# Threshold attention and a SoLU feed-forward on one Trainium2 core: the weights' blocks moved slot by slot instead of unit by unit

## The chip, the core and the metric

The kernel runs on one NeuronCore of one Trainium2 chip. Times are device microseconds of one execution. The engines are named as the profile names them: PE (TensorE matmuls, with PEld for its weight loads), DVE (VectorE), ACT (ScalarE), POOL (GpSimd), and SP (SyncE), which here does nothing but issue DMAs. Each engine works through its own queue of instructions in order; where one needs something of another engine or of a DMA, it waits on a semaphore, and all that stands behind it on that queue waits with it.

## The reference: what is computed

There are 8 batches with 8 heads of 576 positions and 64 columns. All is float32, except that `w_in` and `w_out` reach the kernel as 64-bit floats and are rebuilt by it as float32.

```
scores = q @ k^T / 8                               # per head, 576 x 576
scores = where(scores >= max(scores) - tau, scores, -1e9)
attn   = exp(scores - max) / (sum + 1e-9)
x      = (attn @ v), heads side by side            # 4608 tokens x 512
h      = x @ w_in                                  # 4608 x 1024
solu   = h * softmax(h)
ln     = (solu - mean) / sqrt(var + 1e-6) * g_ln
out    = ln @ w_out                                # 4608 x 512
```

## The kernel before

**Slots, units and rounds.** A *slot* is one step of attention on 128 rows of scores for each of two heads. A batch has 18 slots: for each of `kind` 0 and 1 and each pair of heads `hp` 0 to 3 two slots, `r` = 0 and 1, and at the end of the batch two slots of `kind` 2 with the 64 left-over rows of all heads. There are 144 slots. Two slots that share (batch, kind, hp) make a *unit*; a unit's weights are multiplied with `v` together. The program is one long list written out by the loop that starts in line 914, the scheduler of the toolkit being told to keep that order (line 846). Each turn of the loop is a *round*; round s computes the scores of slot s. Below, unit n is the one with slots 2n and 2n+1, so units 0 to 8 are batch 0, and 9 to 17 are batch 1.

**What a round issues, in order.** First the scores on PE (`scores`, line 437, 16 matmuls), the row maxima on DVE (`maxes`, line 458), thresholding and exponential on ACT (lines 473 and 482). Then `normalise` of the slot of the round before on POOL (lines 489 to 492), and jobs that have become due, among them `ff_norm2` (line 713) and `ff_swap` (line 724): a token tile of the feed-forward, normalised by ACT into `V` and by DVE into `u`, has two quarters exchanged by four SP transfers `V<-u`. Next comes the large PE step of the round. It is a quarter of the feed-forward, in a cycle of four rounds: `h` first half, `h` second half (line 642, 32 matmuls each), `o` first half, `o` second half (line 747, 64 each). Rounds with an `h` step can also take the weights-times-`v` step of one unit (`attend_steps`, line 558, 72 matmuls, written `pv`); rounds with an `o` step take none. After this, `blocks` of the slot of the round before: DVE turns the weights in 32x32 blocks (line 517) and SP moves them. Last in a round come the late jobs, among them `ff_turn` (line 734), in which DVE turns `V` into `uT`: in the steady cycle `ff_swap` stands in the first `h` round, `ff_turn` in the second, and the `o` step of the round after that reads `uT` as its stationary operand. Then come the flips and loads of later `q` and `k` (lines 186 to 189 and 168) and loads of `v` (line 151), all on SP.

**Which rounds multiply a unit.** `pv` of unit n is due in round 2n+4, in a few places one later (line 788), but it is taken in the next `h` round. In batches 2 to 7 the four-round cycle fits the units: of two units, one is taken 3 and one 4 rounds after its second slot. In batch 1 the cycle is not yet in step, and four units, 9, 11, 14 and 16, are taken 5 rounds after their second slot (rounds 24, 28, 34 and 38), just before, in program order, the blocks of the second slot of the unit two further on.

**The tiles T and wT.** `T` holds the turned weights, `wT` the same after the transfers that gather from each quarter of the partitions the halves that `pv` needs. `T` has two buffers of 9216 bytes per partition, `wT` two of the same size, so the transfers of unit n+2 write the buffer that `pv` of unit n reads, and must wait for it. There are two forms:

- batch 0, kinds 0 and 1 (`by_slot`): each slot's half of `T` is moved at once, by one transfer of 288 KB (line 512) and two of 144 KB (line 514), in packets of 2304 bytes. The `wT` buffer is taken at the first slot.
- everything else: DVE fills T with both slots, and only after the second are both moved together, by one transfer of 576 KB and two of 288 KB (lines 526 and 528), or, for kind 2, four of 288 KB (line 533), in packets of 4608 bytes. The `wT` buffer is taken at the second slot.

The functions that the diff touches and what calls them:

Of the kernel before, what the change touches and what calls it, by code (L numbers as in the profile page):

```python
# [8 lines left out]
F32 = mybir.dt.float32  # L9
# [7 lines left out]
P = 128  # L17
# [3 lines left out]
def kernel(  # L21
# [27 lines left out]
    nc = tc.nc  # L49
# [7 lines left out]
    NB = S // 32  # L57
    SCALE = -0.125
    BIG = 3.0e38
    ROWS = (slice(0, 64), slice(64, P))  # L60
# [4 lines left out]
    work = ctx.enter_context(tc.tile_pool(name="work", bufs=2))  # L65
# [24 lines left out]
    NK = S // 64  # L90
# [6 lines left out]
    units = {}  # L97
# [6 lines left out]
    def take(name):  # L104
        tag = pairs_free.pop(0)
        return tag, ps_mm.tile([P, 1024], F32, tag=tag, name=name)
# [76 lines left out]
    def turn_natural(i, nm, a):  # L183
# [3 lines left out]
        for j in range(2):  # L187
            nc.sync.dma_start(
                out=pair(i + j)[nm + "T"][:, 32 * NK * a : 32 * NK * (a + 1)],
                in_=flip[ROWS[j]].rearrange("p g t x -> p g (t x)"),  # L190
            )

    def constants(spread):
        ones = work.tile([P, P], F32, tag="T", name="ones")
        nc.gpsimd.memset(ones[0:1], 1.0)
        nc.gpsimd.memset(lims[0], 0.0)
        nc.scalar.activation(out=ntau, in_=lims[0], func=AF.Exp)
        make_identity(nc, ident)
        nc.gpsimd.memset(mhalf, -0.5)
        nc.gpsimd.memset(mone, -1.0)  # L200
        nc.gpsimd.memset(zero, 0.0)
        for l, e in zip(lims, (916, 896)):
            nc.gpsimd.memset(l, -e * 8388608.0)

        nc.tensor.matmul(out=spread, lhsT=ones[0:1], rhs=tau_row, start=True, stop=True)
        nc.vector.tensor_scalar(
            out=scl, in0=spread, scalar1=0.0, scalar2=SCALE, op0=ALU.is_ge, op1=ALU.mult
        )  # L210
        nc.vector.tensor_scalar(
            out=tau_t, in0=spread, scalar1=0.0, scalar2=104.0, op0=ALU.max, op1=ALU.min
        )
        nc.vector.tensor_scalar(out=ntau, in0=tau_t, scalar1=-1.0, scalar2=None, op0=ALU.mult)
# [141 lines left out]
    def source(i):  # L356
        b, hp = divmod(i, NP)
        return halves[b, hp // 2], 2 * (hp % 2)

    def pair(i):  # L360
        if i not in pairs:
            qT = heads.tile([P, S], F32, tag="qT", bufs=6, name="qT")
            pairs[i] = dict(
                qT=qT,
                kT=heads.tile([P, S], F32, tag="kT", name="kT"),
                qe=heads.tile([P, ST], F32, tag="qe", name="qe"),
            )
        return pairs[i]
# [18 lines left out]
    def keep(room, i, nm, ms, by_act):  # L387
        of = room[:, 0 : 64 * len(ms)].rearrange("p (m x a) -> p m a x", a=2, x=32)
        to = pair(i)[nm + "T"].rearrange("p (a m x) -> p m a x", a=2, m=NK)[:, ms[0] : ms[-1] + 1]
        if nm == "k":  # L390
# [21 lines left out]
    live = {}  # L412
# [83 lines left out]
    def blocks(s):  # L496
        b, kind, hp, r = slots[s]
        key = (b, kind, hp)
        if r == 0:
            by_slot = b == 0 and kind < 2  # L500
            dims = [P, 2, NB, 2, 32] if by_slot else [P, NB, 2, 2, 32]
            units[key] = dict(T=work.tile(dims, F32, tag="T", name="T"), by_slot=by_slot)
        u = units[key]
        T = u["T"]
        if u["by_slot"]:
            for h, w in enumerate(live.pop(s)["w"]):
                nc.vector.transpose(out=T[:, r, :, h], in_=w)  # L507
            if r == 0:
                u["wT"] = work.tile([P, 2, 2, NK, 2, 32], F32, tag="wT", bufs=2, name="wT")
            of = T[:, r].rearrange("p (c m) h x -> p c (m h x)", c=2)  # L510
            to = u["wT"][:, r].rearrange("p g m h x -> p g (m h x)")
            nc.sync.dma_start(out=to[:, 1], in_=of[32:96])
            for half in range(2):
                nc.sync.dma_start(out=to[ROWS[half], 0], in_=of[96 * half : 96 * half + 32])
            return
        for h, w in enumerate(live.pop(s)["w"]):
            nc.vector.transpose(out=T[:, :, r, h, :], in_=w)  # L517
        if r == 0:
            return


        T = T.rearrange("p (c m) r h x -> p c (m r h x)", c=2)
        u["wT"] = wT = work.tile([P, 2, NK, 2, 2, 32], F32, tag="wT", bufs=2, name="wT")
        to = wT.rearrange("p g m r h x -> p g (m r h x)")
        if kind < 2:
            nc.sync.dma_start(out=to[:, 1], in_=T[32:96])
            for half in range(2):
                nc.sync.dma_start(out=to[ROWS[half], 0], in_=T[96 * half : 96 * half + 32])
            return
        for g in range(2):  # L530
            for half in range(2):
                of = 64 * half + 32 * g
                nc.sync.dma_start(out=to[ROWS[half], g], in_=T[of : of + 32])

    def attend_steps(key):
        b, kind, hp = key
        unit = units[key]
        wT = unit["wT"].rearrange("p r g m h x -> p g m r h x") if unit["by_slot"] else unit["wT"]  # L540
        unit["y"] = take("pv")
        _, y = unit["y"]
        y = y.rearrange("p (u n) -> p u n", u=2)

        for e in range(2) if kind == 2 else [None]:
            for m in range(NK):
                for u in range(2):
                    d, h0 = source(b * NP + (hp if e is None else e + 2 * u))
                    for h in range(2):
                        if e is None:  # L550
                            to = y[ROWS[h], u, 0:P].rearrange("p (g r x) -> p g r x", r=2, g=2)
                            rhs = wT[ROWS[u], :, m, :, h]
                        else:
                            to = y[ROWS[h], u, 64 * e : 64 * e + 64].rearrange(
                                "p (g x) -> p g x", g=2
                            )
                            rhs = wT[ROWS[u], :, m, e, h]
                        nc.tensor.matmul(  # L558
                            out=to,
                            lhsT=d["v"][  # L560
                                ROWS[u], (h0 + h - u) % 4, m,
                            ],
                            rhs=rhs,
                            start=m == 0, stop=m == NK - 1,
                        )
                        yield
# [248 lines left out]
    for i in range(2 * NP, NPAIR, 2):  # L815
        b, hf = divmod(i // 2, 2)
# [3 lines left out]
        for nm, pieces_at in zip("qk", ats):  # L820
            for a, at in enumerate(pieces_at):
                at += PER * b
                if b == 2:
                    of = at - 3 - (at in (PER + 7, PER + 9))
                else:
                    of = (at - 3) // 4 * 4
# [19 lines left out]
    with tc.manual_schedule():  # L846
# [16 lines left out]
        weight_load(5, nc.sync)  # L863
        tags, tiles = zip(take("tp"), take("tp"))
        constants(tiles[1][:, 1022:1023])
        turn(tiles[0], 0, "k", range(NK))
        turn(tiles[1], 0, "q", range(4))
# [46 lines left out]
        while True:  # L914
# [92 lines left out]
            if attending is not None and attending[1] == 2 and step is not None:  # L1007
                beside = attend_steps(attending)
# [23 lines left out]
            if attending is not None:  # L1032
                for _ in beside or attend_steps(attending):
                    pass
                attended(attending)
                b, kind, hp = attending
                if kind == 2 and b % 2:
                    ready.append((rnd + 1, [(b // 2,)]))
                elif kind < 2 and hp == NP - 1:
                    ready.append((rnd + 1, [(b, kind, 0), (b, kind, 1)]))  # L1040
            if rnd - 1 in live:
                blocks(rnd - 1)
# [10 lines left out]
            if rnd in pieces:  # L1053
                x = pieces[rnd]
# [52 lines left out]
```

## Time and profile before

| | |
|---|---|
| time, median of 3 runs | 855.23 us (852.27 to 858.17) |
| the profiled execution | 853.01 us, of which the span of the profile is 851.2 us |
| PE busy | 818.8 us (96%) |
| DVE / ACT / POOL busy | 675.2 / 568.7 / 496.3 us |
| DMA, queue of SP | 77298 packets, 165.82 MB, 76.9% of 16 engines' span |
| mean granted TensorE clock | 0.987 |

A busy share is a union of an engine's instructions; DMA shares are the mean of the 16 DMA engines. The rows of groups give line, engine, operation, out<-in and count, then busy time, the mean of one in ns, and the idle time before it with what ended it. A timeline row gives start and duration in us; neighbouring instructions of one kind are merged and counted. Rows with SPq are DMA issues on SP's queue: their duration is the time that SP spent on issuing, and the transfer itself lands later.

### The profile page before, as it was taken

What the parts mean: (1) busy time and instruction counts of PE and PEld (TensorE: products, weight loads), DVE (VectorE), ACT (ScalarE), POOL (GpSimd) and SP (SyncE); (2) the same over time, 40 slices, a digit from 0 to 9 for tenths busy, and PEclk for the clock granted to TensorE, in tenths of its full rate; (3) what the DMA queues carried; (4) which work ended last, traced back from release to release, by engine and by line L of the source; (5) the groups of instructions that cost most, each with busy time, mean ns of one, the idle gap of its engine ahead of it and who ended that gap; (6) DMA issues with size and microseconds to landing.
All of it is one profiled execution on the core that took longest, in us unless ns stands there. A gap on an engine that the chain in (4) does not pass through costs nothing.

```text
span 851.2 us, 36155 instructions
## 1 busy us (share of the span) xinstructions
PE 818.8 (96%) x15363; PEld 625.6 (73%) x15363; DVE 675.2 (79%) x1229; ACT 568.7 (67%) x1123; POOL 496.3 (58%) x945
## 2 busy tenths in 40 slices
PE   6779999999999999999999999999999999999997
PEld 5456678678688777777677777777788888887655
DVE  5999887888788888888688888888888888776461
ACT  6878776867566667666677766666666667775221
POOL 4887646666556556565566666565666655555120
PEclk8899999999999999999999999999999999999999
DMA  9998797888888788887878878987888787655312
GB/s 337 265 260 236 198 223 210 222 220 210 220 225 204 192 208 205 226 214 182 204 184 227 219 176 199 234 210 194 213 202 233 200 187 176 165 135 136 68 39 63
DMA packets 77746, 168.54 MB, mean 198 GB/s; under 512 B 11530, under 2 KB 33042, under 8 KB 77586
## 3 DMA queue, kind: packets, MB, share of 16 engines
q1 hardware_dynamic: 77298, 165.82, 76.9%
q8 instruction: 120, 1.97, 1.0%
q10 hardware_dynamic: 288, 0.43, 0.2%
q14 instruction: 40, 0.33, 0.1%
HBM read 46.14 MB, written 9.44 MB: 65 GB/s over the span
## 4 chain that ended last, share of the span: by engine, by line
PE 84%; DVE 4%; DMA 4%; ACT 2%; issue 2%; POOL 1%; SPq 1%; DVEq 0%; ACTq 0%
PE o_ps L747 28%; PE h_ps L642 22%; PE s_ps L437 15%; PE pv L558 14%; PE h_ps L632 3%; DMA wT<-T 2%; DMA raw<-in_moe_w_out_dram 1%; DVE w L458 1%; PE tp L374 1%; ACT w L473 1%; DVE T L507 1%; SPq L724 1%; ACT w L482 1%; DVE bs L687 1%; DMA k<-in_k_dram 0%
## 5 line engine op out<-in xcount | busy, mean ns | idle before, releaser
L747 PE MATMUL o_ps<-w,uT 64*64 64x256 f32 x4608 | 272.1, 378 | 3.2 <-issue 2.6
L473 ACT ACTIVATE w<-s_ps,nth 128x576 f32<-128x576 f32 x280 | 196.9, 738 | 110.8 <-DVE nth L458 93.9
L747 PEld LDWEIGHTS o_ps<-w,uT 64*64 64x64 f32 x4608 | 226.8, 134 | 54.2 <-ACT xh L588 12.1
L458 DVE CUSTOM_DVE_ANT_0 w<-s_ps,tau_t 128x576 f32<-128x576 f32 x280 | 200.0, 751 | 80.6 <-PE s_ps L437 50.9
L492 POOL TENSOR_SCALAR w<-w,sm 128x576 f32<-128x576 f32 x288 | 220.7, 778 | 14.3
L482 ACT ACTIVATE w<-w,ntau 128x576 f32<-128x576 f32 x288 | 219.5, 766 | 0.0
L642 PE MATMUL h_ps<-w,xh 64*64 64x512 f32 x1728 | 205.7, 589 | 0.0
L517 DVE STREAM_TRANSPOSE T<-w 128x576 f32<-128x576 f32 x256 | 184.3, 754 | 20.3 <-POOL w L492 18.3
L558 PEld LDWEIGHTS pv<-wT,v 64*64 64x64 f32 x5760 | 172.0, 134 | 33.4 <-issue 16.4
L437 PE MATMUL s_ps<-kT,qT 64*64 64x64 f32 (+1 forms) x2048 | 175.6, 416 | 14.9 <-ACT w L473 12.6
L558 PE MATMUL pv<-wT,v 64*64 64x128 f32 (+1 forms) x5760 | 172.1, 261 | 3.9 <-DMA wT<-T 2.3
L642 PEld LDWEIGHTS h_ps<-w,xh 64*64 64x64 f32 x1728 | 112.4, 133 | 70.2 <-issue 36.3
L489 POOL TENSOR_SCALAR sm<-sm 128x2 f32<-128x2 f32 x144 | 33.8, 235 | 187.2 <-ACT w L482 183.5
L490 POOL TENSOR_TENSOR sm<-sm,mone 128x2 f32<-128x2 f32 x144 | 107.7, 748 | 12.0
L437 PEld LDWEIGHTS s_ps<-kT,qT 64*64 64x64 f32 x2048 | 72.7, 136 | 23.3 <-ACT w L473 18.5
L588 ACT COPY xh<-pv 128x256 f32<-128x256 f32 x64 | 25.4, 398 | 75.2 <-PE pv L558 75.2
L708 ACT ACTIVATE V<-u,nb,rs 128x1024 f32<-128x1024 f32 x36 | 44.7, 1241 | 40.5 <-POOL nb L698 33.5
L734 DVE STREAM_TRANSPOSE uT<-V 128x1024 f32<-128x1024 f32 x36 | 44.3, 1230 | 17.5 <-DMA V<-u 16.9
L482 ACT ACTIVATION_READ_ACCUMULATOR w<-w,ntau 128x1 f32 x288 | 55.3, 192 | 0.0
L672 DVE TENSOR_TENSOR u<-h_ps,u 128x1024 f32<-128x1024 f32 x36 | 42.8, 1189 | 8.4 <-ACT u L666 8.4
L713 DVE TENSOR_SCALAR u<-u,rs,nb 128x1024 f32<-128x1024 f32 x36 | 34.5, 958 | 17.6 <-ACT V L708 17.6
L687 DVE BATCH_NORM_STATS2 bs<-u 128x6 f32<-128x512 f32 x72 | 46.1, 683 | 0.1
(81 smaller groups left out, 593.1 us busy)
## 6 DMA issues: line engine op xcount, KB each, us to landing
wT<-T SPq DMA_DIRECT2D x160, 288.0 KB, 6.6
wT<-T SPq DMA_DIRECT2D x56, 576.0 KB, 5.4
v<-in_v_dram SPq DMA_DIRECT2D x16, 576.0 KB, 5.2
V<-u SPq DMA_DIRECT2D x144, 64.0 KB, 3.3
out_dram<-ob SPq DMA_DIRECT2D x71, 128.0 KB, 2.6
q<-in_q_dram SPq DMA_DIRECT2D x28, 288.0 KB, 6.5
k<-in_k_dram SPq DMA_DIRECT2D x27, 288.0 KB, 6.2
qT<-flip SPq DMA_DIRECT2D x48, 144.0 KB, 3.4
```

Source lines behind the costliest of these rows:

```text
L437: nc.tensor.matmul(out=ps[h][ROWS[y], ks], lhsT=lhsT, rhs=d["kT"][ROWS[h], ks], start=True, stop=True,)
L458: nc.vector.tensor_tensor_reduce(out=w, in0=ps[:, 0:S], in1=(zero if loose else tau_t).to_broadcast([P, S]), scale=1.0, scalar=BIG, op0=AL ...
L473: nc.scalar.activation(out=d["w"][x], in_=d["w"][x] if d["loose"] else d["ps"][x][:, 0:S], func=AF.Prelu, bias=d["nth"][x], scale=-1.0, al ...
L482: nc.scalar.activation(out=w, in_=w, func=AF.Exp, bias=ntau, scale=1.0, accum_out=sm[:, x : x + 1])
L490: nc.gpsimd.tensor_tensor(out=sm, in0=sm, in1=mone, op=ALU.pow)
L492: nc.gpsimd.tensor_scalar(out=w, in0=w, scalar1=sm[:, x : x + 1], scalar2=1.0, op0=ALU.mult, op1=ALU.mult)
L517: nc.vector.transpose(out=T[:, :, r, h, :], in_=w)
L558: nc.tensor.matmul(out=to, lhsT=d["v"][ROWS[u], (h0 + h - u) % 4, m,], rhs=rhs, start=m == 0, stop=m == NK - 1,)
L642: mm = nc.tensor.matmul(out=h[ROWS[y], f], lhsT=x[ROWS[r], c, ROWS[y]], rhs=w1_parts[ROWS[r], c, part ^ r], start=part == 0 and c == 0, st ...
L687: nc.vector.bn_stats(out=bs[:, f], in_=u[:, 512 * f : 512 * f + 512])
L708: nc.scalar.activation(out=V, in_=u, func=AF.Identity, bias=nb, scale=rs)
L747: nc.tensor.matmul(out=d["o"][ROWS[z], 512 * (r ^ other) : 512 * (r ^ other) + 256], lhsT=d["uT"][ROWS[r], m].rearrange("p y x -> p (y x)" ...
```

## The change

Every unit now takes the form of the first of the two: `T` becomes a tile of one slot (4608 bytes per partition) with three buffers, DVE turns a slot's weights into it, and the slot is moved at once. `wT` is taken at the first slot of each unit and has one layout throughout. Kind 2 keeps its four transfers, now per slot and half as large. Moved bytes, DVE's turns and PE's matmuls stay in number as they were.

```diff
     def constants(spread):
-        ones = work.tile([P, P], F32, tag="T", name="ones")
+        ones = work.tile([P, P], F32, tag="T", bufs=3, name="ones")
...
         b, kind, hp, r = slots[s]
         key = (b, kind, hp)
         if r == 0:
-            by_slot = b == 0 and kind < 2
-            dims = [P, 2, NB, 2, 32] if by_slot else [P, NB, 2, 2, 32]
-            units[key] = dict(T=work.tile(dims, F32, tag="T", name="T"), by_slot=by_slot)
-        u = units[key]
-        T = u["T"]
-        if u["by_slot"]:
-            for h, w in enumerate(live.pop(s)["w"]):
-                nc.vector.transpose(out=T[:, r, :, h], in_=w)
-            if r == 0:
-                u["wT"] = work.tile([P, 2, 2, NK, 2, 32], F32, tag="wT", bufs=2, name="wT")
-            of = T[:, r].rearrange("p (c m) h x -> p c (m h x)", c=2)
-            to = u["wT"][:, r].rearrange("p g m h x -> p g (m h x)")
+            units[key] = dict(
+                wT=work.tile([P, 2, 2, NK, 2, 32], F32, tag="wT", bufs=2, name="wT")
+            )
+        T = work.tile([P, NB, 2, 32], F32, tag="T", bufs=3, name="T")
+        for h, w in enumerate(live.pop(s)["w"]):
+            nc.vector.transpose(out=T[:, :, h], in_=w)
+        of = T.rearrange("p (c m) h x -> p c (m h x)", c=2)
+        to = units[key]["wT"][:, r].rearrange("p g m h x -> p g (m h x)")
+        if kind < 2:
             nc.sync.dma_start(out=to[:, 1], in_=of[32:96])
             for half in range(2):
                 nc.sync.dma_start(out=to[ROWS[half], 0], in_=of[96 * half : 96 * half + 32])
             return
-        for h, w in enumerate(live.pop(s)["w"]):
-            nc.vector.transpose(out=T[:, :, r, h, :], in_=w)
-        if r == 0:
-            return
-        T = T.rearrange("p (c m) r h x -> p c (m r h x)", c=2)
-        u["wT"] = wT = work.tile([P, 2, NK, 2, 2, 32], F32, tag="wT", bufs=2, name="wT")
-        to = wT.rearrange("p g m r h x -> p g (m r h x)")
-        if kind < 2:
-            nc.sync.dma_start(out=to[:, 1], in_=T[32:96])
-            for half in range(2):
-                nc.sync.dma_start(out=to[ROWS[half], 0], in_=T[96 * half : 96 * half + 32])
-            return
         for g in range(2):
             for half in range(2):
-                of = 64 * half + 32 * g
-                nc.sync.dma_start(out=to[ROWS[half], g], in_=T[of : of + 32])
+                at = 64 * half + 32 * g
+                nc.sync.dma_start(out=to[ROWS[half], g], in_=of[at : at + 32])
...
     def attend_steps(key):
-        wT = unit["wT"].rearrange("p r g m h x -> p g m r h x") if unit["by_slot"] else unit["wT"]
+        wT = unit["wT"].rearrange("p r g m h x -> p g m r h x")
```

## The prediction

> **What bounds the kernel now.** I read the page's head first, then the time by stretches (PE and the other engines, then clock, DMA share and GB/s), then the chain.
>
> ```profile
> PE 818.8 (96%) x15363; PEld 625.6 (73%) x15363; DVE 675.2 (79%) x1229; ACT 568.7 (67%) x1123; POOL 496.3 (58%) x945
> ```
> ```profile
> core 0: us, PE busy (x) PEld busy (x) DVE busy (x) ACT busy (x) POOL busy (x), PEclk, DMA share, GB/s
> 50.00:100.00 50.00, 44.88 (x844) 30.27 (x840) 45.01 (x87) 41.20 (x86) 39.94 (x61) 0.93 0.90 231
> 450.00:500.00 50.00, 50.00 (x939) 36.38 (x935) 42.54 (x76) 35.78 (x72) 32.23 (x65) 1.00 0.84 208
> ```
> ```profile
> 456.61 0.99 PE s_ps L437 x14
> ...
> 478.22 0.99 PE s_ps L437 x14
> ```
>
> From round 17 on PE is the bound: 50.00 us of 50.00 in the stretch from 450, and in the chain a cycle of four rounds repeats after 478.22 - 456.61 = 21.6 us, all of it matmuls. So in the steady cycle no other engine can give time back; it can only take time, by making PE wait. What PE waits for today on account of the tile that the change touches:
>
> ```profile
> PE pv L558 <- DMA wT<-T: 2.3, 4, 1.2
> ```
>
> That is 2.3 us in four waits, the longest, 1.2, in batch 0, where nothing changes. **At most some 1 us can be won** (2.3 - 1.2).
>
> **The change, part by part.**
>
> *DVE's turns.* Same 288 instructions; the new tile has the block stride that batch 0 has already.
>
> ```profile
> L517 DVE STREAM_TRANSPOSE T<-w 128x576 f32<-128x576 f32 x256 | 184.3, 754 | 20.3 <-POOL w L492 18.3
> L507 DVE STREAM_TRANSPOSE T<-w 128x576 f32<-128x576 f32 x32 | 23.5, 766 | 2.2 <-POOL w L492 1.8
> ```
>
> 256 x (766 - 754) ns = 3 us of DVE, which idles a sixth of the steady cycle (42.54 of 50.00 busy): 0 on the path, 3 us if that idle time were gone.
>
> *PE's reads of `wT`.* Four runs of 32 columns in either layout. In batch 0 with the slot layout and in batch 4 with the other, 72 matmuls are busy equally long:
>
> ```profile
> 69.00:72.00 3.00, 2.23 (x72) 2.23 (x72) 1.00 0.90 245
> 454.00:457.00 3.00, 2.20 (x72) 2.16 (x72) 1.00 1.01 293
> ```
>
> 0.03 us for each of 64 units at the most, 2 us; I take 0, since the quick one lies beside a busier DMA.
>
> *SP's issues and the packets.* 56 units of kind 0 and 1 go from 3 to 6 transfers, 8 of kind 2 from 4 to 8: 56 x 3 + 8 x 4 = 200 more on SP, and 64 units have 512 packets of 2304 bytes in place of 256 of 4608.
>
> ```profile
> L528 SPq DMA_DIRECT2D wT<-T x112: 591/1210/3729, 116.4 to 778.0; - x112
> L526 SPq DMA_DIRECT2D wT<-T x56: 570/582/1177, 115.7 to 776.7; - x56
> L514 SPq DMA_DIRECT2D wT<-T x32: 537/598/1347, 18.1 to 97.3; - x32
> L512 SPq DMA_DIRECT2D wT<-T x16: 571/582/775, 17.4 to 95.1; - x16
> ```
> ```profile
> wT<-T SPq DMA_DIRECT2D x160, 288.0 KB, 6.6
> wT<-T SPq DMA_DIRECT2D x56, 576.0 KB, 5.4
> ```
>
> A whole unit costs SP 0.58 + 2 x 1.21 = 3.0 us (medians) today, because the second 288 KB transfer is held up at issue behind the 864 KB in front of it; two half units cost 2 x (0.58 + 2 x 0.60) = 3.6 us. That is +0.6 us for each unit, some 1.2 us in a cycle, on a queue that is rather full:
>
> ```profile
> 451.93 0.57 SPq L526 DMA_DIRECT2D wT<-T  x1
> 452.55 3.01 SPq L528 DMA_DIRECT2D wT<-T  x2
> 455.66 4.09 SPq L724 DMA_DIRECT2D V<-u  x4
> ...
> 472.83 0.57 SPq L526 DMA_DIRECT2D wT<-T  x1
> ```
>
> From the first row's start to the last one's are 20.9 us, and the 19 transfers in them fill 19.3; at 0.6 us each they would need 11.4, so 7.9 us is SP being held up by the DMA engines behind it. With 25 transfers the bare issues are 15.0 us. The bytes are the same, and in batch 0 a mix with the small packets ran at 231 GB/s with a DMA share of 0.90, against 208 needed here, so the hold-ups should shrink with the bursts. And the transfers for which PE soon waits, `V<-u`, then have half as much directly in front of them (the second slot alone), while the first slot's stand behind. I take **0**; the other end is the third rival.
>
> The Trainium skill, "DMA: Bandwidth & Descriptors", section "Anatomy of one DMA — SWDGE (gpsimd) path", gives a transfer a fixed 2.0 us beside bytes / 436 GB/s, and its section "Bandwidth" advises transfers of 1 MiB and more; by that, 200 more would be an estimated 400 us if they stood one behind the other. The landing rows above do not bear that out: 576 KB lands in 5.4 us and 288 KB in 6.6, so the queue and not the piece sets the time, and I give that rule no chance beyond the third rival's.
>
> *The earlier taking of `wT`, a new wait.* The first slot of unit n+2 now writes the buffer of unit n one round earlier than anything did. From batch 2 on that costs little: in the unit at 454 the `pv` starts at 454.67 and ends before 456.61 (the chain), while SP is busy with `V<-u` up to 459.75 anyway. **In batch 1 it does cost.** Unit 9 is multiplied in round 24, but the first slot of unit 11 has its blocks in round 23. SP's queue keeps the program's order, so SP stands at that transfer until `pv` of a later round is done, and everything behind it stands too.
>
> ```profile
> 131.99 1.44 DVE L517 STREAM_TRANSPOSE T<-w 128x576 f32<-128x576 f32 x2
> 139.06 0.27 PE L558 MATMUL pv<-wT,v 64*64 64x128 f32 x1
> 134.15 1.21 SPq L188 DMA_DIRECT2D qT<-flip  x2
> 137.11 2.50 SPq L724 DMA_DIRECT2D V<-u  x4
> 144.01 1.25 DVE L734 STREAM_TRANSPOSE uT<-V 128x1024 f32<-128x1024 f32 x1 [1.13 <-DMA V<-u]
> 146.24 3.68 PE L747 MATMUL o_ps<-w,uT 64*64 64x256 f32 x63
> ```
>
> *Place A, unit 11.* The turned slot is there at 133.43, the `pv` of unit 9 ends at 139.33. Then the slot's three issues, 0.58 + 2 x 0.60 and 0.1 for gaps: 141.2. Behind them in the same order stand the two flips, two loads of `v` and one of `k`, which take 137.11 - 134.15 = 3.0 us up to `V<-u`: 144.2. Four issues, 2.5: 146.7. Today uT starts 144.01 - 139.61 = 4.4 us after the last issue, directly on the landing: 151.1. It takes 1.25, and `o` starts 0.1 later, at 152.4 instead of 146.24: **+6.2 us**.
>
> ```profile
> 188.05 0.27 PE L558 MATMUL pv<-wT,v 64*64 64x128 f32 x1
> 184.23 1.20 SPq L188 DMA_DIRECT2D qT<-flip  x2
> 185.47 0.60 SPq L151 DMA_DIRECT2D v<-in_v_dram  x1
> 186.81 3.16 SPq L724 DMA_DIRECT2D V<-u  x4
> 192.46 1.20 DVE L734 STREAM_TRANSPOSE uT<-V 128x1024 f32<-128x1024 f32 x1
> 195.40 3.72 PE L747 MATMUL o_ps<-w,uT 64*64 64x256 f32 x64
> ```
>
> *Place C, unit 16*, which waits for unit 14. The slot is turned before the round's flips are issued at 184.23; `pv` ends at 188.32, three issues 190.2, flips and `v` 186.07 - 184.23 = 1.8: 192.1, `V<-u` 2.5: 194.6. Today uT starts 192.46 - 189.97 = 2.5 after the last issue without a wait, so landing takes at most that: 197.1, end of uT 198.3, `o` at 198.4 instead of 195.40: **+3.0 us**.
>
> *Units 13 and 18* wait in the same way for units 11 and 16, but there uT ends well before its `o`:
>
> ```profile
> 169.23 1.24 DVE L734 STREAM_TRANSPOSE uT<-V 128x1024 f32<-128x1024 f32 x1
> 173.80 1.56 PE L747 MATMUL o_ps<-w,uT 64*64 64x256 f32 x24
> 213.34 1.20 DVE L734 STREAM_TRANSPOSE uT<-V 128x1024 f32<-128x1024 f32 x1
> 221.82 0.38 PE L747 MATMUL o_ps<-w,uT 64*64 64x256 f32 x2
> ```
>
> 3.3 and 7.3 us to spare: I take 0. Three buffers of `T` keep the distance to the next writer at three slots, as now: 0.
>
> *Sum.* 6.2 + 3.0, less 0.5 (half of the 1 us that can be won: where a unit's second half stands behind a late `V<-u`, its wait stays), is **+8.7 us**. The profiled execution took 853.01 us (span 851.2), so 861.7; on the median of the runs, 855.23, which stands 2.2 above it, **863.9**. PE has no idle time behind batch 1 in which to make this good. That uT's lateness, through DVE's maxima behind it, holds up the next scores as well is not in the sum; nothing shows it, and it has 3.5 us of `o` as cover, so I allow 0 to 0.5 us a place. The landing is the unknown; for line 724 (`V<-u`) the trace has:
>
> ```profile
> DMA to landing us min/median/max: 1.9/3.3/6.7
> ```
>
> Counted from the start of the last of the four issues (146.1 and 194.0), 1.9 gives +3.1 and +1.8, 6.7 gives +7.9 and +6.6 by the same steps; with the 1 us won or not, and 0 to 1 for the scores, the sum lies between +3.9 and +15.5.
>
> **The rivals.**
>
> 1. *Not slower: the transfers in front of `V<-u` do not hold it.* Mechanism at places A and C: the allocator puts the transfer that waits behind `V<-u`, or gives it a free buffer, or `V<-u` lands within the room there is. It decides if uT comes less than 1.0 us late at A (146.24 less 145.26, its end today) and 1.7 at C (195.40 less 193.66). For it: the DMA in front is half as much. Against: only two buffers exist, units 9 and 10 hold both at 133 us, and SP's rows are in program order throughout. Price: -1.0, 852 on the profiled execution, 854 on the median.
> 2. *As forecast but smaller*: landing near the quick end, +4 to +7: 859 to 862.
> 3. *SP becomes the bound.* If the 7.9 us of hold-ups in a cycle stay while the issues grow to 15.0, SP needs 22.9 and some 1.3 for gaps (25 of 0.05, as between 452.50 and 452.55), 24.2 against 21.6: 2.6 us for each of about 27 cycles between 200 and 780 us, 70 us, 925. It decides once the hold-ups stay above 21.6 - 16.3 = 5.3. For it: SP is busy for 19.3 of 20.9 us. Against: the 231 GB/s of batch 0. Half-way forms (`V<-u` 0.5 us late beyond its room in each cycle) give 10 to 15 us more, 875 to 880.
>
> **How the numbers follow.** A measurement of this kernel can tell about 1% from no change (its three runs spread by 0.7%). Forecast (+7 to +15.5): 0.50. Rival 2: 0.15. Rival 1: 0.15. Rival 3 and its half-way forms: 0.20, half of it above 880. 1% is 8.6 us: the forecast's upper two thirds and all of rival 3 are beyond it, 0.35 + 0.20 = 0.55; the rest is within, 0.43, with 0.02 for faster, since only 1 us is there to be won. The range goes from rival 1's 854, with 1 us less for a quick run, to the half-way forms: 853 to 880.
>
> **What would show it.** In the changed kernel SP has a wait of some 6 us at the first slot of unit 11 (near 133) and 5 at unit 16, ended by PE `pv`; DVE uT waits some 7 and 4 us for `V<-u` there; PE has a gap before line 747 of about 6 and 3 us. Elsewhere the cycle stays 21.6 us, and DVE's waits for `V<-u` after 300 us become shorter. The forecast is wrong if the cycle lengthens (rival 3), if no gap stands before `o` in batch 1 (rival 1), or if scores wait for late flips instead.

## The result, and the profile after

The changed kernel takes **860.94 us** (median of 10 runs, 859.33 to 867.02), the kernel before beside it 854.29 (10 runs, 850.41 to 858.17): ratio 1.0087, 95% interval 1.0058 to 1.0117. The prediction was 863.9, in a range of 853 to 880. The profiled execution of the changed kernel is the longest of its ten, 867.02 us with a span of 865.2. In its program the lines that matter have moved: DVE's turns are L505, the transfers of blocks L509 and L511 (kind 2: L516), `pv` is L541, `V<-u` L707, uT L717, `o` L730.

The page of the changed kernel, engine totals and the queue of SP's transfers:

```profile
PE 824.4 (95%) x15363; PEld 573.7 (66%) x15363; DVE 675.8 (78%) x1229; ACT 569.1 (66%) x1123; POOL 496.9 (57%) x945
...
q1 hardware_dynamic: 96882, 165.84, 71.6%
```

As many matmuls, as many bytes, 19584 packets more (96882 against 77298: 16384 because 4608-byte packets became two, and 16 small ones for each of the 200 further transfers), and yet the DMA engines' share is down from 76.9% to 71.6%. The waits of the changed kernel (engine, line, what it waited for: us in total, times, longest) show what is new; SP's own list has the other end of it:

```profile
DVE uT L717 <- DMA V<-u: 18.6, 5, 8.4
...
PE o_ps L730 <- DVE uT L717: 8.7, 2, 6.0
```
```profile
SPq L509 <- PE pv L541: 16.7, 8, 5.9
```

In the trace of before neither PE's wait for uT nor SP's for `pv` at a first slot exists. Place A in the timeline of the changed kernel (start, duration, instruction, idle time before it and what ended it; the view ends at 160 us, so its last row has only 16 of the 64 `o` matmuls):

```profile
144.99 0.57 SPq L509 DMA_DIRECT2D wT<-T  x1
145.60 1.35 SPq L511 DMA_DIRECT2D wT<-T  x2
147.06 1.22 SPq L188 DMA_DIRECT2D qT<-flip  x2
148.33 1.12 SPq L151 DMA_DIRECT2D v<-in_v_dram  x2
149.50 0.43 SPq L168 DMA_DIRECT2D k<-in_k_dram  x1
150.03 2.49 SPq L707 DMA_DIRECT2D V<-u  x4
...
156.91 1.25 DVE L717 STREAM_TRANSPOSE uT<-V 128x1024 f32<-128x1024 f32 x1 [8.41 <-DMA V<-u]
...
158.31 1.99 PE L730 MATMUL o_ps<-w,uT 64*64 64x256 f32 x16 [6.00 <-DVE uT L717]
```

This is the queue of the prediction, row by row: first slot of unit 11 behind `pv`, flips, `v`, `k`, `V<-u`, landing, uT, `o`. Place C:

```profile
202.67 0.57 SPq L509 DMA_DIRECT2D wT<-T  x1
...
206.57 2.48 SPq L707 DMA_DIRECT2D V<-u  x4
...
212.28 1.25 DVE L717 STREAM_TRANSPOSE uT<-V 128x1024 f32<-128x1024 f32 x1 [3.82 <-DMA V<-u]
...
213.67 5.37 PE L730 MATMUL o_ps<-w,uT 64*64 64x256 f32 x64 [2.68 <-DVE uT L717]
```

PE stands still for 6.00 and 2.68 us, after SP's waits for `pv` of 5.9 us at unit 11 and 4.0 at unit 16. What was not foreseen is behind the gaps. Time by stretches in the changed kernel (PE, PEld, DVE, ACT, POOL busy, then granted clock, DMA share, GB/s):

```profile
155.00:160.00 5.00, 1.69 (x16) 1.16 (x20) 3.08 (x4) 0.70 (x1) 0.00 (x0) 0.59 0.86 231
160.00:165.00 5.00, 5.00 (x72) 3.17 (x68) 3.75 (x7) 3.44 (x8) 2.10 (x6) 0.72 0.74 184
...
210.00:215.00 5.00, 2.32 (x35) 1.22 (x28) 2.72 (x3) 0.72 (x2) 2.02 (x3) 0.90 0.75 178
215.00:220.00 5.00, 5.00 (x73) 3.63 (x71) 4.11 (x8) 3.81 (x8) 1.63 (x4) 0.76 0.93 246
```

The clock is halved for a while after each gap: (0.41 + 0.28) x 5 us x 2 = 6.9 us at half speed at A, (0.10 + 0.24) x 5 x 2 = 3.4 us at C. 64 `o` matmuls take 5.37 us there, 3.69 at full clock.

Behind batch 1 the kernel is better than before, not equal. Scores of the same rounds in the changed kernel's timeline, and the stretch from 300 to 700 us, first before, then after:

```profile
456.57 1.19 PE L437 MATMUL s_ps<-kT,qT 64*64 64x64 f32 x16
...
478.17 1.19 PE L437 MATMUL s_ps<-kT,qT 64*64 64x64 f32 x16
```
```profile
300.00:700.00 400.00, 397.76 (x7670) 309.49 (x7666) 331.88 (x600) 277.60 (x551) 242.37 (x472) 1.00 0.83 207
```
```profile
300.00:700.00 400.00, 400.00 (x7692) 277.56 (x7688) 336.64 (x606) 280.50 (x555) 243.76 (x474) 1.00 0.78 209
```

The cycle is still 21.60 us, but 2.2 us of PE idle time are gone in this stretch, at a smaller DMA share. Set side by side by the start of each round's first score matmul, the two profiled executions differ so:

| stretch | after less before, us | forecast |
|---|---|---|
| up to round 26 (batch 0, its loads and weights) | +5.6 | 0 |
| place A (rounds 26 to 27) | +8.65 | +6.2 |
| rounds 27 to 36 | +1.1 | 0 |
| place C (36 to 37) | +4.6 | +3.0 |
| round 37 to round 140 | -5.7 | -0.5 |
| sum | +14.3 | +8.7 |

The first row is only in part the change's. Six of the kernels here, this one among them, have the same program up to the blocks of round 23; their profiled executions stand at -2.6 to +5.6 at round 26, 1.8 on the mean. So 3.8 of the 6 us by which the profiled execution is above the median are scatter in this stretch, and sums of single executions can't be held against medians to better than some us. The 1.8 have a place: between rounds 18 and 20 the changed kernel loses 3.1 us, where the first slot of unit 8 (kind 2 of batch 0) now has its transfers in front of the loads of `q` and `k` of batch 1. Of eight kernels with these transfers early, six lose 1.5 to 3.3 us there and two nothing (1.7 on the mean); of four without, three lose nothing and the one with transfers cut by partitions 1.7.

The third row is a place of its own too, between rounds 35 and 36. POOL waits for a `q` load that SP issued 3.9 us later, against the start of round 35, than before; a POOL instruction that PE waits for (`mark`) comes 1.6 us later, and the next scores 1.1:

```profile
204.39 3.66 PE L625 MATMUL h_ps<-w,xh 64*64 64x512 f32 x32 [0.79 <-POOL mark L110]
```

Kernels in which the first slots of units 11, 13, 16 and 18 are put off lose nothing there; those with unit 11 alone and unit 16 alone put off lose 1.1 and 0.8. That SP's 2.1 us at unit 13 make this load late would fit, but no run has unit 13 alone.

### The profile page after: what moved, and what is told of

Same layout as the page of the kernel before. It is cut to its first block, busy times and chain, and to the rows that moved or that the text cites. A ratio compares the mean times of both kernels' runs of the same rounds, so it can differ in the third digit from the quotient of the medians.

```text
span 865.2 us, 36638 instructions
## 1 busy us (share of the span) xinstructions
PE 824.4 (95%) x15363; PEld 573.7 (66%) x15363; DVE 675.8 (78%) x1229; ACT 569.1 (66%) x1123; POOL 496.9 (57%) x945
## 3 DMA queue, kind: packets, MB, share of 16 engines
q1 hardware_dynamic: 96882, 165.84, 71.6%
## 4 chain that ended last, share of the span: by engine, by line
PE 80%; DMA 7%; DVE 4%; issue 3%; ACT 2%; SPq 2%; POOL 1%; DVEq 0%; ACTq 0%
PE o_ps L730 27%; PE h_ps L625 21%; PE pv L541 14%; PE s_ps L437 13%; PE h_ps L615 3%; DMA wT<-T 3%; DMA k<-in_k_dram 1%; ACT w L473 1%; DMA q<-in_q_dram 1%; DVE w L458 1%; DMA V<-u 1%; DVE T L505 1%; ACT w L482 1%; DMA v<-in_v_dram 1%; SPq L707 1%
## 5 line engine op out<-in xcount | busy, mean ns | idle before, releaser
L730 PE MATMUL o_ps<-w,uT 64*64 64x256 f32 x4608 | 269.1, 382 | 11.6 <-DVE uT L717 8.7
L730 PEld LDWEIGHTS o_ps<-w,uT 64*64 64x64 f32 x4608 | 215.7, 135 | 78.0 <-issue 28.7
L492 POOL TENSOR_SCALAR w<-w,sm 128x576 f32<-128x576 f32 x288 | 221.2, 781 | 14.3
L505 DVE STREAM_TRANSPOSE T<-w 128x576 f32<-128x576 f32 x288 | 209.3, 761 | 23.5 <-POOL w L492 17.1
L625 PE MATMUL h_ps<-w,xh 64*64 64x512 f32 x1728 | 200.1, 589 | 0.8 <-POOL mark L110 0.8
L541 PEld LDWEIGHTS pv<-wT,v 64*64 64x64 f32 x5760 | 162.5, 135 | 42.4 <-issue 29.2
L437 PE MATMUL s_ps<-kT,qT 64*64 64x512 f32 (+1 forms) x2048 | 166.1, 418 | 13.8 <-ACT w L473 12.4
L541 PE MATMUL pv<-wT,v 64*64 64x128 f32 (+1 forms) x5760 | 165.9, 262 | 2.7 <-DMA wT<-T 1.7
L625 PEld LDWEIGHTS h_ps<-w,xh 64*64 64x64 f32 x1728 | 85.8, 133 | 96.7 <-issue 84.5
L437 PEld LDWEIGHTS s_ps<-kT,qT 64*64 64x64 f32 x2048 | 62.9, 137 | 23.1 <-ACT w L473 17.8
L717 DVE STREAM_TRANSPOSE uT<-V 128x1024 f32<-128x1024 f32 x36 | 43.6, 1211 | 18.6 <-DMA V<-u 18.6
L649 ACT ACTIVATE u<-h_ps,hm 128x1024 f32<-128x1024 f32 x36 | 40.2, 1117 | 19.8 <-DVE hm L640 13.8
```

Of the source, the lines that this page charges most:

```text
L437: nc.tensor.matmul(out=ps[h][ROWS[y], ks], lhsT=lhsT, rhs=d["kT"][ROWS[h], ks], start=True, stop=True,)
L492: nc.gpsimd.tensor_scalar(out=w, in0=w, scalar1=sm[:, x : x + 1], scalar2=1.0, op0=ALU.mult, op1=ALU.mult)
L505: nc.vector.transpose(out=T[:, :, h], in_=w)
L541: nc.tensor.matmul(out=to, lhsT=d["v"][ROWS[u], (h0 + h - u) % 4, m,], rhs=rhs, start=m == 0, stop=m == NK - 1,)
L625: mm = nc.tensor.matmul(out=h[ROWS[y], f], lhsT=x[ROWS[r], c, ROWS[y]], rhs=w1_parts[ROWS[r], c, part ^ r], start=part == 0 and c == 0, st ...
L717: nc.vector.transpose(out=uT, in_=d["V"].rearrange("p y (m x) -> p m y x", x=32))
```

## Experiments

### The wait, and its two places

Three kernels put transfers off and change nothing else: DVE turns the first slot as before, its three transfers are issued together with the second slot's. In the first this holds for units 11, 13, 16 and 18 (those whose first slot finds both `wT` tiles unread), in the second for unit 11 only (`key == (1, 0, 2)` in place of `len(units) > 2`), in the third for unit 16 only (`key == (1, 1, 3)`).

```diff
...
+        units[key]["kept"].append((r, T))
+        if r == 0 and len(units) > 2:
+            return
+        if "wT" not in units[key]:
+            units[key]["wT"] = work.tile([P, 2, 2, NK, 2, 32], F32, tag="wT", bufs=2, name="wT")
+        for x in units[key]["kept"]:
+            move(key, *x)
...
```

> The changed kernel, but where the unit two before has not yet been multiplied when a unit's first slot is turned (units 11, 13, 16 and 18, batch 1), the first slot's transfers are issued together with the second's, a round later and behind V<-u. Still 200 more transfers than before, in 2304-byte packets. The wait theory (SP stands at wT in front of V<-u in units 11 and 16, and all of the loss is there): both gaps before the o step vanish, and the time falls by the shifts that the changed kernel's profile shows there, 8.6 and 5.6 us, to 861 - 14 = 847, 0.8% under the kernel before. The rival (many small transfers cost a little everywhere): only part of it is at these places, the time stays at 857 to 861, above the kernel before.

> The changed kernel with the first slot's transfers put off for unit 11 alone. Wait theory: the 6 us gap before the o step at unit 11 goes, with it the half clock behind it; unit 16's stays. 861 - 8.6 = 852. The rival of small transfers everywhere: 861, less 0 to 2.

> The changed kernel with the first slot's transfers put off for unit 16 alone. Wait theory: the 2.7 us gap at unit 16 goes, unit 11's stays: 861 - 5.6 = 855. The rival: 861, less 0 to 2. If the two places weren't independent, e2 and e3 would not add up to e1.

| put off | median, us | ratio to before (855.57) | gap at A | gap at C |
|---|---|---|---|---|
| all four | 848.46 | 0.9915 (0.9885 to 0.9946) | none | none |
| unit 11 | 852.39 | 0.9955 (0.9932 to 0.9978) | none | 2.65 |
| unit 16 | 857.59 | 1.0015 (0.9987 to 1.0042) | 6.51 | none |

The waits of the second and of the third kernel, a place each:

```profile
PE o_ps L737 <- DVE uT L724: 2.6, 1, 2.6
```
```profile
PE o_ps L737 <- DVE uT L724: 6.5, 1, 6.5
```

The three ran side by side, so each place has its price in time, not only in one trace: A 857.59 - 848.46 = **9.1 us**, C 852.39 - 848.46 = **3.9 us**, against 8.65 and 4.6 in the table above (units 13 and 18 are still early in the second and the third kernel, so what they cost is in both prices). With all four put off the kernel is 7.1 us faster than before. 9.1 + 3.9 - 7.1 = 5.9 us is what the whole change should cost; it costs 6.65. In the kernel with all four put off, `V<-u` no longer stands behind the moved blocks at place A (its timeline):

```profile
139.98 1.87 SPq L714 DMA_DIRECT2D V<-u  x3
141.95 0.62 SPq L518 DMA_DIRECT2D wT<-T  x1
142.61 1.25 SPq L520 DMA_DIRECT2D wT<-T  x2
...
146.80 1.25 DVE L724 STREAM_TRANSPOSE uT<-V 128x1024 f32<-128x1024 f32 x1 [1.68 <-DMA V<-u]
...
148.49 3.68 PE L737 MATMUL o_ps<-w,uT 64*64 64x256 f32 x62
```

From the other side, the kernel before with the slot form in batch 1 alone:

```diff
-            by_slot = b == 0 and kind < 2
+            by_slot = b <= 1 and kind < 2
```

> The kernel before, with the slot-wise form (batch 0's) given to kinds 0 and 1 of batch 1 as well: 24 more transfers in place of 200, T still two buffers of a unit. Wait theory: both gaps are there in full, and none of what the changed kernel wins later (5.7 us at batch ends): 854 + 13 to 15 = 867 to 869, slower than the fully changed kernel. The rival: an eighth of the difference, 854 to 856.

866.74 us, ratio 1.0115 (1.0087 to 1.0144): the change in one batch of the seven costs more than the whole of it, though its 11.2 us above the kernel before fall short of the 13 to 15 that were expected. In its trace A costs 8.6 us, but C, expected in full, only 0.8:

```profile
204.47 3.68 PE L747 MATMUL o_ps<-w,uT 64*64 64x256 f32 x64 [0.59 <-DVE uT L734]
```

SP waits for `pv` there too, but `V<-u` lands sooner: uT starts 1.5 us after SP is done with the four issues, 3.2 in the changed kernel. The gap is 0.59 us and no half clock follows. So the wait decides that `V<-u` comes late, and the landing, 1.7 us apart in these two traces, how much of it PE sees. Nothing is given back afterwards (+1.4 us from round 39 on, where the changed kernel has -5.7). So batch 1 holds the loss and the later batches a gain.

### Where the gain comes from

Is it the early start of half of the transfers, or the smaller pieces? The next kernel has the pieces of the change, but from batch 1 on always issues both slots together, after the second, as the kernel before did.

```diff
...
+        if r == 0 and (b > 0 or kind == 2):
+            return
...
```

> Transfers and packets as in the changed kernel (half as large, 200 more than before), but from batch 1 on, and for every unit of kind 2, both slots of a unit are issued together after the second slot, as the kernel before does. No transfer is issued early, so no new wait. It parts what the version with the four units put off won over the kernel before (848.5 against 855.6): if the smaller packets and transfers won it, 847 to 850; if the earlier start of the first slot did, 853 to 856. The rival that 200 small transfers cost by themselves: over 857.

849.01 us, ratio 0.9936 (0.9906 to 0.9966). That is as much as with the early start (848.46, ratio 0.9915), so the early start has no part in the gain that these intervals could show. Pieces differ from those of before in two things, half the bytes in a transfer and half the bytes in a packet. The kernel before, with every transfer cut in two by partitions, has the first without the second, but each piece comes from half as many partitions:

```diff
-        if kind < 2:
-            nc.sync.dma_start(out=to[:, 1], in_=T[32:96])
-            for half in range(2):
-                nc.sync.dma_start(out=to[ROWS[half], 0], in_=T[96 * half : 96 * half + 32])
-            return
+        for y in range(2):
+            if kind < 2:
+                at = 32 + 32 * y
+                nc.sync.dma_start(out=to[ROWS[y], 1], in_=T[at : at + 32])
+                for half in range(2):
+                    p, at = 64 * half + 32 * y, 96 * half + 16 * y
+                    nc.sync.dma_start(out=to[p : p + 32, 0], in_=T[at : at + 16])
+                continue
...
```

> The kernel before with each transfer of a unit's blocks cut in two by partitions: six transfers a unit (eight for the third kind) after the second slot, all with 4608-byte packets as before. Beside the kernel that moved both slots together in small pieces (849.0 us) it differs in the packets alone: the same number of transfers, the same bytes in each. If the gain comes from the smaller packets: no gain, 854 to 858 us, and the landing of a piece stays above 4.5 us. If it comes from transfers of half the bytes: 847 to 850 us, as there.

**894.54 us**, ratio 1.045 (1.0422 to 1.0478). Halving the transfers in this way wins nothing and loses 39 us, a price that neither side had expected. The rows of the 144 KB pieces (duration of an issue on SP in ns, min/median/max), first with both slots together in small packets, then with the cut transfers, and under it what PE and DVE then wait for:

```profile
L520 SPq DMA_DIRECT2D wT<-T x256: 537/604/2209, 17.6 to 778.2; - x128
```
```profile
L531 SPq DMA_DIRECT2D wT<-T x224: 576/1095/2522, 119.7 to 821.7; - x112
```
```profile
DVE uT L737 <- DMA V<-u: 69.7, 32, 4.3
PE pv L561 <- DMA wT<-T: 17.3, 21, 2.9
```

The same number of issues with the same bytes each: 604 ns with 2304-byte packets, 1095 with 4608-byte ones. From 300 to 700 us SP spends 370 us on issuing in the kernel with the cut transfers, 321 in the other, 325 in the kernel before, 315 in the changed one. So twice as many transfers fit on SP where the hold-ups go with the small pieces. In the cut kernel they do not go, and PE is idle for 15.7 of the 400 us. In the same two traces a 2304-byte packet takes 134 ns of a DMA engine on the mean, a 4608-byte one 362. The kernel before has both sizes in one trace, 130 and 300 ns: more than twice as much for twice the bytes. One reservation: the cut pieces also come from half as many partitions (32 and 16 rows), and that has a price of its own, 362 ns for a packet in place of 300. So the 39 us are not the price of the packet size alone, and that the gain comes from smaller packets and not from smaller transfers is argued from the times of the packets, not shown: large packets in half transfers from all the partitions were not run.

How near SP's bound is shows the kernel with the four put off and each transfer of kinds 0 and 1 cut in two by partitions, small packets kept, 12 transfers a unit:

```diff
...
-            nc.sync.dma_start(out=to[:, 1], in_=of[32:96])
             for half in range(2):
-                nc.sync.dma_start(out=to[ROWS[half], 0], in_=of[96 * half : 96 * half + 32])
+                nc.sync.dma_start(out=to[ROWS[half], 1], in_=of[32 + 32 * half : 64 + 32 * half])
+            for half in range(2):
+                for x in range(2):
+                    p, o = 64 * half + 32 * x, 96 * half + 16 * x
+                    nc.sync.dma_start(out=to[p : p + 32, 0], in_=of[o : o + 16])
...
```

> The version with the four units put off (848.5), each transfer of kinds 0 and 1 cut once more in two by partitions: 12 transfers a unit in place of 6, packets of 2304 bytes as they are. In a cycle of four rounds SP then has 37 transfers to issue; at 0.6 us and 0.05 between them 24 us against PE's 21.6. If SP is a queue that becomes the bound once its bare issues exceed PE's cycle, the cycle goes to 24 us or more and the time to 848 + 27 x 2.4 = 910 or more. If the hold-ups of SP take up the further issues as they did for the first 200, it stays under 855.

996.4 us, ratio 1.1645 (1.1592 to 1.1698). Its stretches and SP's rows:

```profile
400.00:500.00 100.00, 90.21 (x1616) 63.52 (x1612) 68.32 (x123) 56.11 (x114) 48.83 (x95) 0.93 0.76 172
```
```profile
503.82 1.21 SPq L519 DMA_DIRECT2D wT<-T  x2
505.07 3.31 SPq L523 DMA_DIRECT2D wT<-T  x4
```

SP issues one transfer after the other, 556 from 300 to 700 us at 0.65 us on the mean, which with 0.05 between them fill 390 of the 400 us. PE is idle for a tenth of the stretch shown, and the clock falls with it. A cycle takes 25.7 us, more than the 24 of the bare issues, and a 2304-byte packet 156 ns in place of 134, so cutting by partitions adds to it here as well. The third rival's mechanism exists; the change stays on the near side of it.

### The half clock

Matmuls that nobody reads behind the scores of round 26 keep PE busy in the gap at A: 60 of them in the first kernel, 24 in the second (`range(6)`); the profile counts two instructions for each.

```diff
+        if s == 26:
+            for x in range(15):
+                for h in range(2):
+                    for y in range(2):
+                        nc.tensor.matmul(
+                            out=ps[h][ROWS[y], S:1024], lhsT=ident[ROWS[h], ROWS[h]],
+                            rhs=d["kT"][ROWS[h], 0 : 1024 - S], start=True, stop=True,
+                        )
```

> The changed kernel with 60 more matmuls (64x64 by 64x448, results read by nobody) on PE behind the scores of round 26, where PE waits 6 us for uT: some 5.6 us of work in a gap that is there anyway. At this place the changed kernel loses 8.6 us with a gap of 6.0. If the other 2.6 us are the halved clock behind the gap (granted 0.5 for 6.8 us), the clock stays at 1.0 here, the loss at the place falls to about 6 and the time to 858.5; unit 16's place keeps its own. If not, the time stays at 861 or rises.

863.87 us, ratio 1.0114 (1.007 to 1.0158): missed. The timeline says why; the added matmuls (L445) outlast the gap:

```profile
147.92 11.71 PE L445 MATMUL s_ps<-kT,ident 64*64 64x448 f32 x120
152.56 1.25 DVE L725 STREAM_TRANSPOSE uT<-V 128x1024 f32<-128x1024 f32 x1 [8.01 <-DMA V<-u]
159.20 3.68 PE L738 MATMUL o_ps<-w,uT 64*64 64x256 f32 x62
```

uT is done at 153.81, and `o` waits 5.4 us more for PE itself.

> The changed kernel with 24 matmuls whose result nobody reads behind the scores of round 26 (60 of them took 11.7 us and held the o product up themselves; 24 take some 4.7 us, less than the gap of 6.0 us). Half-clock theory (of the 8.65 us that place A costs, about 2.6 us are the slow matmuls behind the gap, 6.8 us at a granted clock of 0.5): the clock stays near 1.0 from 155 to 165 us, rounds 26 to 27 take about 10.5 us instead of 13.1, and the time is about 858.5 us. Rival (the rest of the 8.65 us is a chain behind the late uT and no matter of the clock): 13 us from round 26 to 27, and 861 us.

863.04 us, ratio 1.0094 (1.0063 to 1.0126): missed in time. In the profiled execution (858.22 us) the mechanism is there:

```profile
143.61 4.95 PE L445 MATMUL s_ps<-kT,ident 64*64 64x448 f32 x48
148.88 1.25 DVE L725 STREAM_TRANSPOSE uT<-V 128x1024 f32<-128x1024 f32 x1 [8.63 <-DMA V<-u]
150.27 3.69 PE L738 MATMUL o_ps<-w,uT 64*64 64x256 f32 x64 [1.71 <-DVE uT L725]
```
```profile
150.00:155.00 5.00, 4.65 (x80) 3.68 (x84) 5.00 (x10) 3.54 (x7) 1.01 (x3) 1.00 0.85 211
```

The clock is 1.00, `o` takes 3.69 us, and A costs 6.7 us instead of 8.65. At C the same execution has a gap that happens to be followed by the full clock:

```profile
203.84 3.68 PE L738 MATMUL o_ps<-w,uT 64*64 64x256 f32 x64 [3.08 <-DVE uT L725]
```

C costs 3.3 us with this gap of 3.08, and 4.6 in the changed kernel with one of 2.68 and a half clock. That the half clock is the other 2 us of A is thus shown in one execution each; in the medians, 863.04 against 860.94, not measured side by side and with spreads of 8 to 10 us, it is not seen, and what those added matmuls cost elsewhere stays open.

### Another way out, and the best kernel

If SP waits because `wT` has only two tiles, a third should do as well as putting off. Room for it comes from `T`, which goes from three tiles to two.

```diff
-                wT=work.tile([P, 2, 2, NK, 2, 32], F32, tag="wT", bufs=2, name="wT")
+                wT=work.tile([P, 2, 2, NK, 2, 32], F32, tag="wT", bufs=3, name="wT")
...
-        T = work.tile([P, NB, 2, 32], F32, tag="T", bufs=3, name="T")
+        T = work.tile([P, NB, 2, 32], F32, tag="T", bufs=2, name="T")
```

> The changed kernel with three tiles for the moved blocks (wT) instead of two, and two for the turned ones (T) instead of three. The program order is left as it is and the first slot's transfers go early, as in the changed kernel. Wait theory (the changed kernel loses its time where a transfer into wT waits on SP for the PV product of an earlier unit, with V<-u queued behind it): with a third tile the PE gap of 6.0 us in unit 11 and that of 2.7 us in unit 16 are gone, and the time falls to that of the kernel with the transfers put off, 847 to 849 us. Rival (the loss comes from issuing a first slot's transfers early, among the loads of q, k and v, whatever they wait for): the kernel stays near 858 to 861 us.

853.87 us, ratio 0.9969 (0.9951 to 0.9987): between the two. Both gaps are gone from its trace (A 0.1 us, C 0), so early issue in itself does not make them; 5 us of the expected gain are missing. The last kernel is the changed one with two `T` tiles and nothing else:

> The changed kernel with two of the half-size T tiles instead of three, and nothing else; a DVE turn of a round then waits until the transfers of the round but one before have landed. The kernel with a third wT tile had two T tiles too and ran at 853.9 us, some 5 us above the kernel with the transfers put off. If the second T tile is what those 5 us were for: 865 to 867 us here. If it costs nothing, and issuing early has a price of its own in the kernel with the third wT tile: 859 to 862 us, as with three.

867.28 us, ratio 1.0147 (1.0106 to 1.0187): 6 us more than with three, as the first reading had it. From 130 to 230 us, first the changed kernel, then this one:

```profile
DVE T L505 <- DMA wT<-T: 0.6, 1, 0.6
```
```profile
DVE T L505 <- DMA wT<-T: 8.9, 4, 3.4
```

With two tiles DVE waits for the landing of an earlier slot, and rounds 26 to 39 cost 18.3 us against 14.4. So the second `T` tile has a price of the size that is missing above; where the kernel with three `wT` tiles pays it was not seen, since its profiled execution (849.73 us) was its quickest.

Last, the first kernel with unit 8's first slot put off as well, `if r == 0 and (len(units) > 2 or key == (0, 2, 0))`:

> The version with the four units put off (848.5), with the first slot of unit 8 (kind 2 of batch 0) put off as well. In that version PE loses 1.8 us between rounds 18 and 20, where it waits for q and k of batch 1, whose loads now stand behind unit 8's first transfers in SP's queue. If that order is the cause, these 1.8 us go: 846.7. If not, 848.5.

847.71 us, ratio 0.9926 (0.9893 to 0.9959). Between rounds 18 and 20 its trace loses nothing against before, as was expected, where the first kernel loses 1.8 us. It is quicker than both kernels of the case, by 7.7 us than before and by 13 than the changed one; in time it cannot be told from the first, 848.46.

## Why the prediction was right, point by point

- **PE-bound cycle**: held; 21.60 us on both sides.
- **DVE's turns and PE's reads at 0**: held; 675.2 and 675.8 us of DVE, and no lengthening of the cycle.
- **200 more transfers at 0, because the hold-ups shrink**: held, and more than held. The changed kernel's 256 second and third pieces take 604 ns at the median where 1210 were needed:

```profile
L511 SPq DMA_DIRECT2D wT<-T x256: 537/604/1862, 18.4 to 792.2; - x128
```
```profile
wT<-T SPq DMA_DIRECT2D x320, 144.0 KB, 3.7
wT<-T SPq DMA_DIRECT2D x128, 288.0 KB, 3.8
```

  In the cycle from 457 us, 25 issues fill 18.7 us where 19 filled 19.3, so of 7.9 us of hold-ups 3.7 are left, below the 5.3 from which the third rival decides. The experiments add that the smaller pieces do this; that it is their packets is argued from 130 and 300 ns a packet.
- **Place A, +6.2**: the mechanism and its size were right. Less the 5.63 us by which the trace is late at that point, uT starts at 151.28 (forecast 151.1) and `o` at 152.68 (152.4), 6.4 us later than before. **Place C, +3.0**: less 15.41, by which the trace is late at round 36, `o` starts at 198.26 (198.4), 2.9 later. That fits the forecast better than the steps do: of the 15.41 us 1.1 arise only between rounds 35 and 36, the round in which SP's wait ends. Less 14.31, by which the trace is late before it, `V<-u` is issued at 192.26 (192.1), uT starts at 197.97 (197.1, a landing 0.9 longer) and `o` at 199.36, 4.0 later, and 1.1 of these are PE's own lateness. The term that was left out comes after that: PE works on at half clock from 158.31 to some 162.8 and for 3.4 us at C, which loses 2.2 and 1.7 us. A is thus 8.65 and C 4.6.
- **Units 13 and 18 at 0**: held for the chain that was worked out; no gap stands before `o` there. But SP stands for 2.1 us at each, and the prediction asked only what that does to uT, not to the loads of `q` behind it: the 1.1 us before round 36 probably come from there. Nor did it ask this of unit 8, whose first transfers stand in front of loads too: some 1.7 us between rounds 18 and 20, not in every execution.
- **At most 1 us to be won, 0.5 taken**: this was mis-sized. From round 37 on 5.7 us come back, 5.4 with the wait removed. What was wrong is the step from PE's waits for `wT` to the whole gain. Waits from 220 to 850 us, before and then after:

```profile
DVE uT L734 <- DMA V<-u: 15.8, 13, 4.5
...
PE s_ps L437 <- issue: 1.8, 1, 1.8
PE o_ps L747 <- issue: 0.9, 1, 0.9
PE pv L558 <- issue: 0.5, 1, 0.5
```
```profile
DVE uT L717 <- DMA V<-u: 6.4, 3, 4.0
...
PE s_ps L437 <- issue: 0.3, 1, 0.3
```

  DVE's waits for `V<-u` became shorter, as forecast, but they never held PE. The time comes back in five rounds, 6.0 us less 0.6 that round 47 loses: 1.2 us at round 40, where PE had waited for `wT`, and 1.1, 0.7, 2.1 and 0.9 at rounds 41, 56, 76 and 92. Three of these are the "issue" stalls above, in which PE waited for nothing that the profile shows; the fourth (round 56) has no gap in the rows. The prediction passed over them because no tile was named in them. In the kernel with batch 1 alone, whose later batches move large packets, stalls of 2.3 and 1.5 us stand at 420 and 516 us. That they are PE's instructions arriving late behind the large packets would fit the fetches in the trace (a packet of the instruction queue overlaps the stall at 411 us) but is only argued.

The terms that were left out or mis-sized, +3.9 for the clock, some +1.1 and +1.7 for the late loads and -5.2 for the gain, nearly cancel; that the forecast of 863.9 is only 3 us from 860.94 is partly luck.

## What to carry to other kernels

When a buffer is taken earlier, look for the instruction that now waits on an in-order queue, write down what stands behind it, and follow that up to the bound engine: here two waits in the whole program cost some 13 us, and putting those transfers off one round turns a slower kernel into a faster one. Price a transfer on a busy queue by its hold-ups as well as by its issue; smaller pieces paid here, and cutting the same pieces by partitions did not. To a PE gap of some us add the slow matmuls that can follow it.

## What was not expected of the hardware

- **A gap is followed by a half clock.** After 6.00 us of idle PE the granted clock was 0.5 for 6.9 us, after 2.68 us for 3.4 us; a gap of 3.08 us at C in the kernel with 24 added matmuls was followed by none. The Trainium skill, "TensorE: Matmul & The Clock Gate", Part 1, says that half rate comes after at least one idle window of about 3.4 us, in windows that run on by themselves. The steps of 3.4 us agree with that; the gap of 2.68 us is shorter than a window and halved the clock all the same, and there the measurement decides.
- **Smaller packets cost the DMA engines less.** Twice as many packets for the moved blocks, equal bytes, and q1's share falls from 76.9% to 71.6%; from 300 to 700 us the share is 0.78 instead of 0.83 at 209 instead of 207 GB/s. In the kernel before, one trace with both sizes, a packet of 2304 bytes takes 130 ns on the mean and one of 4608 bytes 300; why more than twice as long, the runs do not say.
- **Cutting by partitions is dear.** 894.54 us with large packets, 996.4 with small ones. The Trainium skill, "DMA: Bandwidth & Descriptors", section "Rules for kernel authors", advises against two transfers to disjoint halves of the partitions, since they share the same engines; both runs agree. The same table advises to join many small transfers into a large one: twice the transfers, moved together, ran at 849.01 us against 855.40, but with packets of half the size, so the runs do not decide on that advice by itself.
